# Attention and an expert layer on one core: a new planner for the instruction order, and the expert rows in two groups

## The chip, the cores and the metric

The kernel runs on one core of one Trainium2 chip. The metric is the device time of one execution in microseconds (us). The kernel before takes 981.07 us, the median of 3 runs (979.69 to 981.55).

## What is computed

Attention over 4 batches, 8 heads, 1152 keys and 64 channels, with neighbouring query rows averaged in pairs (576 query rows a batch), and then a two-layer expert network on the 2304 rows of 512 channels:

```python
q_pool = q.reshape(B, H, S // 2, 2, D).mean(axis=3)
scores = np.matmul(q_pool, k.transpose(0, 1, 3, 2)) / np.sqrt(D)
attn = softmax(scores)
x = np.matmul(attn, v).transpose(0, 2, 1, 3).reshape(B * 576, H * D)
h = x @ w_in                                   # 512 -> 2048
g = np.where(h > 0, h, np.exp(np.minimum(h, 0)) - 1)
out = g @ w_out                                # 2048 -> 512
```

Every fp32 operand of a matmul is held as a high and a low fp16 half under a power-of-two scale, and a product is the sum of three partial products.

## The kernel before

**Units, pairs and steps.** A batch is a unit, and a unit has four pairs of heads. A pair has nine steps: four tiles of 128 rows for each head, and a ninth step with the last 64 rows of both heads. So there are 36 steps a unit and 144 in all. One step (`attention`, from line 626) is a chain: the scores on PE (L643, L649) into the only PSUM tile `s`; the scale and row maximum on DVE (L655); the exponential on ACT (L661); the row sum and its reciprocal (L666, L669); the high half of the probabilities on POOL (L672) or ACT (L680); the low half on DVE (L675); and a DMA transpose from SP's queue that carries both halves from an `ep` buffer (3 of them) into a `pT` buffer (2 of them) (L699). In a "slow" step ACT makes the high half and POOL makes the low half in two instructions (L683, L689); every second one of the first 40 steps is slow. After two steps PE multiplies with V (L736, L742), and ACT and DVE add the result into `x32` (L754, L759), of which there is one buffer.

**Preparation of a pair** (`prep`, L336): loads of q, k and v, absolute maxima on ACT, a maximum over the partitions with two small PE matmuls (`across`, L314), the halves, a DMA transpose of q into `qT` (L439) with three copies behind it (L445, L448), and one of k into `kT` (L451). `kT`, `qT` and `v16` have two buffers each, so a pair can be prepared while one other pair is in work.

**Weights** (`weights`, L494): 8 groups of w_in and 8 of w_out arrive as 64-bit words. DVE decodes the two halves of a group in six instructions (L520, L524, L529, each for both halves), ACT finds the maximum, and the halves are scaled and split (L574, L577, L583).

**Experts** (`experts`, L773), once for each unit, when its last step is in `x32`: two maxima over `x32` (L786), one scale for all 576 rows, the halves of x (L821, L826), and then two row groups of 256 and 320 rows. In each, the first layer is 192 matmuls (L850), with ACT, POOL and DVE behind each result (L858 to L897), and the second layer is 96 or 144 matmuls (L917), with the output from SP's queue (L938).

**What orders the work.** Nothing runs in the order of the source. `Plan.run` (L79) is a list scheduler that runs when the program is built. Every task has an engine, an assumed duration and a key (a due time from the constants `CFG`); some have a second engine that they may go to. The planner keeps a time at which each engine is free, gives the free engine the ready task with the lowest key for which the buffers can be had, and so writes out a fixed order for PE, DVE, ACT, POOL and SP. The chip follows that order on each engine and waits on semaphores where the assumed times are wrong. A DMA has an assumed hold of the queue and a latency, and PE has a factor of 1.45 for unit 0.

Of the kernel before, what the change touches and what calls it, by code (L numbers as in the profile page):

```python
# [17 lines left out]
CFG = dict(LOADS=39538, PLM=2, NS=40, WI0=17116, WIT=12317, WO0=235211, WOT=4483, T0=4000, T1=2284, M0=8135, M1=33164, KS=15043, KM=7701, KE=39223, KH=2922, KL=-6882, KV=6859, KN=7241, KX=17067, KO=35556, PEN=0, W0L=-22914, WIN=1000, PD=2498,  # L18
)

# [17 lines left out]
class Plan:  # L38


    LAT = {"PE": 55.0, "DVE": 35.0, "ACT": 35.0, "POOL": 100.0, "DMA": 0.0}
# [37 lines left out]
    def run(self):  # L79
# [7 lines left out]
        free = {e: 0.0 for e in engines}  # L87
        wait = {e: [] for e in engines}
        events = [0.0]
# [5 lines left out]
        now = 0.0  # L95
        while done < len(self.tasks):
            if not events:
                left = sorted((t for t in self.tasks if t.end is None), key=lambda t: (t.key, t.n))
                raise RuntimeError("no task can be placed: " + "; ".join(
                    f"{t.eng} {t.emit.__name__} {t.left} {[(b.tag, b.slot) for b in t.bufs]}" for t in left[:12]))  # L100
            now = heapq.heappop(events)
            while events and events[0] <= now:
                heapq.heappop(events)
            again = True
            while again:
                again = False
                for e in engines:
                    if free[e] > now:
                        continue
                    best = None  # L110
                    for t in sorted((t for t in wait[e] if t.ready <= now), key=lambda t: (t.key, t.n)):
                        if e != t.eng:
                            ahead = sum(
                                o.dur for o in wait[t.eng]
                                if o.eng == t.eng and o.ready <= now + CFG["WIN"] and (o.key, o.n) < (t.key, t.n)
                            )
                            if now + t.ways[e][0] + CFG["PEN"] > max(free[t.eng], now) + ahead + t.dur:
                                continue
# [14 lines left out]
                    hold, lat = t.dur if isinstance(t.dur, tuple) else (t.dur, self.LAT[e])  # L133
                    free[e] = now + hold
                    t.start, t.end = now, now + hold + (lat if e == "DMA" else 0.0)
                    heapq.heappush(events, free[e])
                    heapq.heappush(events, t.end)
                    for kid in t.kids:
                        kid.left -= 1
                        extra = 60.0 if e == "DMA" else self.LAT[kid.eng]  # L140
                        kid.ready = max(kid.ready, t.end + extra)
                        if kid.left == 0:
                            for o in kid.ways:
                                wait[o].append(kid)
                        heapq.heappush(events, kid.ready)
                    order.append(t)
                    done += 1
                    again = True
        self.span = now
# [12 lines left out]
def attention_moe_kernel(  # L162
# [37 lines left out]
    pool("sm", 4, [128, 16], F32)  # L200
# [6 lines left out]
    pool("us", 2, [128, 16], F32)  # L207
# [4 lines left out]
    pool("wm", 2, [128, 4], F32)  # L212
# [10 lines left out]
    def act(n):  # L223
        return 0.9 * n + 190.0

    def actp(n):
        return 0.85 * n + 130.0

    def dve(n):
        return 1.2 * n + 200.0  # L230

    def dvp(n):
        return 1.07 * n + 170.0

    def pol(n):
        return 0.8 * n + 460.0

    def pol2(n):
        return 2.0 * n + 330.0

    def mm(n, cold=False):
        return (n / 1.55 if cold else n / 2.4) + 14.0

    LOADS, PLM = CFG["LOADS"], CFG["PLM"]
# [24 lines left out]
    for u in units:  # L269
        u.first = len(steps)  # L270
        u.t0 = now
        for p in range(NP):
            pr = Rec()
            pr.u, pr.p, pr.i, pr.t0 = u, p, len(pairs), now
            pr.steps = []
            pairs.append(pr)
            jobs = [(h, t) for h in range(2) for t in range(u.nt)] + ([(None, u.nt)] if u.lo else [])
            for h, t in jobs:
# [4 lines left out]
                now += CFG["T0"] if u.i == 0 else CFG["T1"]  # L283
        u.t1 = now
# [29 lines left out]
    def across(src, n, key, after, bufs, take):  # L314
# [13 lines left out]
        t1 = plan.add("PE", 300.0, key, turn, after, [xp] + bufs)  # L328
        t2 = plan.add("DVE", 600.0, key, most, [t1], [xp, xr])
        t3 = plan.add("PE", 350.0, key, back, [t2], [xp, xr])  # L330
        return plan.add("DVE", 700.0, key, lambda: take(xp.ap[:, 256:256 + n]), [t3], [xp] + bufs)
# [4 lines left out]
    def prep(pr, t0, t1):  # L336
# [35 lines left out]
        def halves(n, kh, kl, dst_h, dst_l, src, j, after, bufs):  # L372
# [3 lines left out]
            return plan.add("DVE", dve(n), kl, f, [h], bufs, [("POOL", pol(n) + pol2(n), g)])  # L376
# [33 lines left out]
        tq = plan.add("DMA", (1600.0, 2500.0), lk - 10.0, load_q, (), [q32])  # L410
# [4 lines left out]
        if old is None:  # L415
# [4 lines left out]
            tk = plan.add("DMA", (1500.0, 2500.0), lk, load(k, k32), (), [k32])  # L420
            tv = plan.add("DMA", (1500.0, 2500.0), lk + 1, load(v, v32), (), [v32])
# [33 lines left out]
        qt = plan.add("DMA", (1400.0, 2500.0), key[8], q_t, [ql], [qn, qT])  # L455
        qw = plan.add("DMA", (1000.0, 2000.0), key[9], q_lo, [qt], [qT])
        pr.qs = plan.add("DMA", (500.0, 2000.0), key[9], q_hi, [qw], [qT])
        if old:
            pr.kdone = [plan.add("DMA", (1500.0, 2500.0), lk + 2, plain(k_f, lambda: old[0]), [old[4]], [kT])]
            pr.vdone = [plan.add("DMA", (1500.0, 2500.0), lk + 3, plain(v_f, lambda: old[1]), [old[5]], [v16])]  # L460
            return
        kl = halves(1152, key[6], key[7], k_h, k_l, k_s, 1, [sc, sums[2]], [kn, k32, sm])
        pr.kdone = [plan.add("DMA", (2500.0, 2500.0), key[9], k_t, [kl], [kn, kT])]
        pr.vdone = [halves(1152, key[11], key[12], v_h, v_l, v_s, 2, [sc], [v16, v32, sm])]
        if sum(o.b == b for o in units) > 1:
            kd = dr.tile([128, 2 * S], F16, name=f"kd{p}")
            vd = dr.tile([128, 2 * S], F16, name=f"vd{p}")
            kw = plan.add("DMA", (1500.0, 2500.0), key[15], plain(lambda: kd, k_f), pr.kdone, [kT])
            vw = plan.add("DMA", (1500.0, 2500.0), key[15], plain(lambda: vd, v_f), pr.vdone, [v16])
            kept[b, p] = (kd, vd, sm, pr.sc, kw, vw)  # L470

    for pr in pairs:
        if pr.i == 0:
            prep(pr, -9000.0, 0.0)
        else:
            prev = pairs[pr.i - 1]
            prep(pr, prev.t0 - 2000.0, pr.t0 - 4000.0)
# [16 lines left out]
    def weights(which, g, t0, t1):  # L494
# [5 lines left out]
        for s in range(2):  # L500
# [7 lines left out]

            lds.append(plan.add("DMA", (1350.0, 2700.0), CFG["W0L"] + s if g + which == 0 else t0 - 14000.0 + s, load, (), [raws[s]]))

# [5 lines left out]
        def dec():  # L516
            us_ = [u.ap.bitcast(U32) for u in us]
            w = [raw_words(r) for r in raws]
            for s in range(2):
                nc.vector.tensor_scalar(  # L520
                    us_[s], w[s][:, :, 1], 5, 2, op0=ALU.logical_shift_left, op1=ALU.logical_shift_right
                )
            for s in range(2):
                nc.vector.scalar_tensor_tensor(  # L524
                    out=us_[s], in0=w[s][:, :, 1], scalar=0xC0000000, in1=us_[s],
                    op0=ALU.bitwise_and, op1=ALU.bitwise_or,
                )
            for s in range(2):
                nc.vector.scalar_tensor_tensor(  # L529
                    out=dst(s), in0=w[s][:, :, 0], scalar=29, in1=us_[s],  # L530
                    op0=ALU.logical_shift_right, op1=ALU.bitwise_or,
                )

        def osum():
            for s in range(2):
                to = mo[:, 2 * g + s:2 * g + s + 1] if which else wm[0].ap[:, s:s + 1]
# [444 lines left out]
```

## Time and profile before

| | us |
|---|---|
| median of 3 runs | 981.07 |
| the profiled execution's own time | 977.62 |
| its span, first to last instruction | 975.8 |
| end of the attention steps of units 0, 1, 2, 3 | 278.7, 483.7, 687.2, 871.0 |
| from the end of unit 3's steps to the end of the span | 104.8 |

Times in the profile count from the span's first instruction. An end of a unit's steps is read where DVE starts the second of the two maxima over `x32` (L786), which needs the last result of the unit. A busy share averages over stages with different limits, so the stages between these times are read one by one. PEclk is the granted clock of TensorE, where 1.00 is 2.4 GHz and 0.5 is 1.2 GHz.

### The profile page before, as it was taken

What the parts mean: (1) busy time and instruction counts of PE and PEld (TensorE: products, weight loads), DVE (VectorE), ACT (ScalarE), POOL (GpSimd) and SP (SyncE); (2) the same over time, 40 slices, a digit from 0 to 9 for tenths busy, and PEclk for the clock granted to TensorE, in tenths of its full rate; (3) what the DMA queues carried; (4) which work ended last, traced back from release to release, by engine and by line L of the source; (5) the groups of instructions that cost most, each with busy time, mean ns of one, the idle gap of its engine ahead of it and who ended that gap; (6) DMA issues with size and microseconds to landing.
All of it is one profiled execution on the core that took longest, in us unless ns stands there. A gap on an engine that the chain in (4) does not pass through costs nothing.

```text
span 975.8 us, 14669 instructions
## 1 busy us (share of the span) xinstructions
PE 745.6 (76%) x5271; PEld 416.6 (43%) x5271; DVE 747.6 (77%) x1200; ACT 627.9 (64%) x1093; POOL 519.0 (53%) x422
## 2 busy tenths in 40 slices
PE   0364464654258989889769997989698999999997
PEld 0122132322126645544346444544365455458563
DVE  5797989899789978788778776887877789845150
ACT  3576786666476868776557666865677778734260
POOL 4373867477579963783247634771276247505130
PEclk9998575556659999999979998999799999999999
DMA  7599899899956989999977989799888698640000
GB/s 238 134 212 228 190 199 254 184 227 222 271 109 126 177 156 184 171 177 184 183 148 137 206 163 193 132 203 190 172 174 172 132 176 135 123 94 7 22 2 27
DMA packets 434057, 156.94 MB, mean 161 GB/s; under 512 B 395840, under 2 KB 414272, under 8 KB 433984
## 3 DMA queue, kind: packets, MB, share of 16 engines
q1 hardware_dynamic: 433984, 156.01, 78.6%
q8 instruction: 41, 0.67, 0.3%
q14 instruction: 32, 0.26, 0.1%
HBM read 45.09 MB, written 4.72 MB: 51 GB/s over the span
## 4 chain that ended last, share of the span: by engine, by line
PE 32%; DMA 21%; DVE 12%; POOL 6%; issue 2%; ACT 2%; SPq 2%; DVEq 0%; POOLq 0%; ACTq 0%
DMA pT<-ep 16%; PE r L917 12%; PE r L850 8%; DVE ep L655 5%; PE r L736 4%; PE s L643 3%; DVE ep L675 3%; PE r L742 2%; PE s L649 2%; DMA kT<-kn 2%; DMA qT<-qn 1%; DMA q<-in_q_dram 1%; POOL ep L672 1%; ACT ep L661 1%; DVE tmp L871 1%
## 5 line engine op out<-in xcount | busy, mean ns | idle before, releaser
L655 DVE TENSOR_SCALAR_CACHE_REDUCE ep<-s,sm 128x1152 f32<-128x1152 f32 x133 | 188.0, 1414 | 80.1 <-DMA pT<-ep 52.2
L661 ACT ACTIVATE ep<-ep,nm 128x1152 f32<-128x1152 f32 x133 | 166.5, 1252 | 98.7 <-DVE ep L655 86.1
L850 PE MATMUL r<-x,wi 128*128 128x256 f16 (+1 forms) x1536 | 201.9, 290 | 9.3 <-DVE x L759 3.1
L643 PE MATMUL s<-kT,qT 128*128 128x512 f16 (+3 forms) x480 | 122.3, 370 | 113.1 <-DVE ep L655 88.9
L675 DVE SCALAR_TENSOR_TENSOR ep<-ep,nm 128x1152 f16<-128x1152 f32 x118 | 193.5, 1642 | 9.2 <-POOL ep L672 6.3
L917 PE MATMUL r<-wo,g 128*128 128x512 f16 (+1 forms) x864 | 174.8, 380 | 0.5 <-DVE tmp L871 0.3
L850 PEld LDWEIGHTS <-wi 128*128 128x128 f16 x1536 | 148.1, 99 | 60.1 <-issue 18.4
L736 PE MATMUL r<-pT,v 128*128 128x256 f16 (+1 forms) x864 | 100.8, 268 | 61.7 <-DMA pT<-ep 49.4
L672 POOL TENSOR_SCALAR ep<-ep,nm 128x1152 f16<-128x1152 f32 x52 | 73.2, 1408 | 104.2 <-DVE nm L669 102.5
L866 POOL TENSOR_SCALAR tmp<-tmp,us 128x320 f32<-128x320 f32 (+1 forms) x96 | 79.6, 830 | 90.4 <-ACT tmp L861 85.6
L680 ACT ACTIVATE ep<-ep,nm 128x1152 f16<-128x1152 f32 x81 | 101.3, 1251 | 31.0 <-DVE nm L669 30.7
L643 PEld LDWEIGHTS <-qT 128*128 128x128 f16 (+1 forms) x480 | 44.8, 106 | 174.8 <-issue 135.3
L917 PEld LDWEIGHTS <-g 128*128 128x128 f16 (+1 forms) x864 | 73.1, 100 | 88.9 <-issue 9.3
L736 PEld LDWEIGHTS <-v 128*128 128x128 f16 x864 | 68.8, 105 | 93.6 <-issue 47.7
L871 DVE SCALAR_TENSOR_TENSOR tmp<-r,wk,tmp 128x320 f32<-128x320 f32 (+1 forms) x96 | 58.0, 611 | 33.4 <-POOL tmp L866 33.2
L649 PE MATMUL s<-kT,qT 64*128 64x512 f16 (+3 forms) x480 | 80.8, 370 | 0.0
L754 ACT ACTIVATE x<-r,sm 64x256 f32<-64x256 f32 (+1 forms) x96 | 39.9, 415 | 47.3 <-PE r L742 45.4
L893 POOL TENSOR_SCALAR g<-tmp 128x320 f16<-128x320 f32 (+1 forms) x55 | 46.7, 850 | 35.8 <-DVE tmp L871 33.4
L742 PE MATMUL r<-pT,v 128*64 128x256 f16 (+1 forms) x864 | 65.5, 274 | 0.0
L858 ACT ACTIVATE tmp<-r 128x320 f32<-128x320 f32 (+1 forms) x96 | 46.3, 484 | 26.5 <-PE r L850 25.0
L889 POOL TENSOR_TENSOR g<-tmp,g 128x320 f16<-128x320 f32 (+1 forms) x54 | 56.8, 1058 | 4.8 <-ACT g L885 3.0
L861 ACT ACTIVATE tmp<-tmp,us 128x320 f32<-128x320 f32 (+1 forms) x96 | 57.7, 609 | 1.5
(136 smaller groups left out, 1029.2 us busy)
## 6 DMA issues: line engine op xcount, KB each, us to landing
k<-in_k_dram SPq DMA_DIRECT2D x16, 576.0 KB, 4.9
v<-in_v_dram SPq DMA_DIRECT2D x16, 576.0 KB, 4.9
q<-in_q_dram SPq DMA_DIRECT2D x32, 256.0 KB, 3.4
qT<-qT SPq DMA_DIRECT2D x48, 144.0 KB, 2.8
g<-in_moe_w_in_dram SPq DMA_DIRECT2D x13, 512.0 KB, 5.4
g<-in_moe_w_out_dram SPq DMA_DIRECT2D x13, 512.0 KB, 4.8
out_dram<-tmp SPq DMA_DIRECT2D x16, 256.0 KB, 2.5
pT<-ep SPq DMA_TRANSPOSE x133, 4.8
```

The source lines that it names most:

```text
L643: nc.tensor.matmul(s.ap[rows, c, 0:n], pr.qT.ap[:, 0, j, rows], keys[c], start=True, stop=False, skip_group_check=True,)
L649: nc.tensor.matmul(s.ap[rows, c, 0:n], pr.qT.ap[r, 1, j, rows], keys[c][r], start=False, stop=True, skip_group_check=True,)
L655: nc.vector.tensor_scalar(e_(), s.ap.rearrange("p a b -> p (a b)")[:, 0:S], pr.sm.ap[:, 12:13], None, op0=ALU.mult, op1=ALU.min, accum_out ...
L661: nc.scalar.activation(out=e_(), in_=e_(), func=AF.Exp, bias=nm.ap[:, 0:1], scale=-1.0, accum_out=nm.ap[:, 2:3],)
L672: nc.gpsimd.tensor_scalar(p_(0), e_(), nm.ap[:, 3:4], 1.0, op0=ALU.mult, op1=ALU.mult)
L675: nc.vector.scalar_tensor_tensor(out=p_(1), in0=e_(), scalar=nm.ap[:, 3:4], in1=p_(0), op0=ALU.mult, op1=ALU.subtract)
L680: nc.scalar.activation(out=p_(0), in_=e_(), func=AF.Copy, scale=nm.ap[:, 3:4])
L736: nc.tensor.matmul(x.ap[:, os], vt[:, order[c]].rearrange("p e d -> p (e d)"), pT.ap[:, c, cs], start=(c == 0), stop=False, skip_group_che ...
L742: nc.tensor.matmul(x.ap[r0:r0 + 64, os], vt[:, order[c], 0], pT.ap[:, NCH + c, cs], start=False, stop=(c >= NCH - 2), skip_group_check=True,)
L850: nc.tensor.matmul(hp.ap[:, f * n:(f + 1) * n], w[:, a, c, (f0 + f) * 128:(f0 + f + 1) * 128], x16.ap[:, e, c, g0:g0 + n], start=(i == 0), ...
L866: nc.gpsimd.tensor_scalar(en.ap[:, :m], en.ap[:, :m], -1.0, us.ap[:, 5:6], op0=ALU.add, op1=ALU.mult)
L917: nc.tensor.matmul(op.ap[r0:r0 + tn, :], gt[qd].ap[:, a, fi, o:o + tn], w_out16(f // 2)[:, e, f % 2, :], start=(i < 128 // tn), stop=(i >= ...
```

## The change

**The planner.** `Plan.run` becomes an event simulation. A task's remaining work is worked down at a rate: DVE and POOL slow each other down while DVE runs a task marked `Port` (rate 0.72 or 0.55), PE runs at 0.57 in a window after little use, and a DMA (`Move`) holds the queue for a first duration and the transfer path for a second one, with 2 us of flight; the transposes of `pT` and `kT` hold the queue until the path is free. Nearly all assumed durations and all `CFG` constants are replaced, with own constants for unit 0 (names that end in 0). On the chip none of this is executed: it changes the order on the engines and the choice of engine where a task has two.

**Steps.** The slow steps become every fourth of the first 36 (`PLM0=4`, `NS0=36`), and none later (`PLM=0`). In each unit the last two pairs are interleaved: four steps of pair 2 (the first two tiles of both heads), four of pair 3, then the five others of pair 2 and the five others of pair 3.

**Experts in two groups with own scales.** `experts` is called for each group; group 0 (256 rows) depends only on the tiles 0 and 1 of each head, so on step 26 of 36. Each group has its own maxima, `across` and scale; `us` gets a third buffer. Both groups share the one `x16` buffer.

**Weights.** The decode is a task for each half; it waits for the low half of the first pair's keys (`first_keys`). The maxima go straight to their columns, and `wm` is now only a token of which there is one, so that one group's maxima and scale are done before those of the next.

```diff
-CFG = dict(LOADS=39538, PLM=2, NS=40, WI0=17116, WIT=12317, ...
+    LOADS=84962, WI0=22119, WIT=12449, WO0=250979, WOT=5600, T0=3996, T1=1105, M0=11183,
...
+    KE0=53762, KH0=-8737, KL0=-4366, KV0=9486, KX0=32985, PLM0=4, NS0=36, PLM=0,
+    M2=18442, DP=0, PA=-86, PB=4000,
...
+            if d is not None and p is not None and isinstance(d.dur, Port):
+                return 0.72 if isinstance(p.dur, Port) else 0.55
+            return 1.0
...
+                    if e == "DMA":
+                        moved = max(now + rest[e], max(moved, now) + t.dur.far)
+                        heapq.heappush(landing, (moved + self.FLIGHT, t.n, t))
+                        rest[e] = (moved - now if t.dur.hold else rest[e]) + 90.0
...
+        early = [(h, t) for h in range(2) for t in range(2)]
+        late_ = [(h, t) for h in range(2) for t in range(2, u.nt)] + [(None, u.nt)]
+        turns = [(pr, early + late_) for pr in mine[:-2]] + [(pr, early) for pr in mine[-2:]] + [(pr, late_) for pr in mine[-2:]]
...
+            td = plan.add("DVE", Port(2000.0), t0 + s, dec, [lds[s], first_keys], [raws[s], us[s]] + to)
...
-        slow = st.i < CFG["NS"] and st.i % PLM == PLM - 1
+        every = K("PLM", u)
+        slow = every and st.i % every == every - 1 and (u.i > 0 or st.i < CFG["NS0"])
...
-        tt = plan.add("DMA", (CFG["PD"], 2200.0), t0, ptr, [tl], [ep, pT])
+        tt = plan.add("DMA", Move(2690.0, 2150.0, True), t0, ptr, [tl], [ep, pT])
...
+        u.xdone[0 if st.h is not None and st.t < 2 else 1].append(plan.add("DVE", 400.0 if n == 256 else 490.0, ...
...
-    def experts(u, t0, t1):
-        us, x16 = plan.buf("us"), plan.buf("x16")
+    def experts(u, gi, t0, t1):
+        us, x16 = plan.buf("us"), u.x16
+        g0, n = u.groups[gi]
...
-        if u.i + 1 < len(units):
-            experts(u, u.t1 + CFG["M0"], units[u.i + 1].t1 + CFG["M1"])
...
+        u.x16 = plan.buf("x16")
+        ends = units[u.i + 1].ready if u.i + 1 < len(units) else [u.t1 + 100000.0, u.t1 + 200000.0]
+        experts(u, 0, u.ready[0] + CFG["M0"], u.ready[1] + CFG["M2"])
+        experts(u, 1, u.ready[1] + CFG["M2"], ends[0] + CFG["M1"])
```

## Rows read from the trace of the kernel before

**Rows 1.** The page, part 1: busy us, share of the span, instructions.

```profile
PE 745.6 (76%) x5271; PEld 416.6 (43%) x5271; DVE 747.6 (77%) x1200; ACT 627.9 (64%) x1093; POOL 519.0 (53%) x422
```

**Rows 2.** The page, part 2: busy tenths in 40 slices, and granted clock.

```profile
PE   0364464654258989889769997989698999999997
...
DVE  5797989899789978788778776887877789845150
...
PEclk9998575556659999999979998999799999999999
```

**Rows 3.** Windows by stage: busy us (instructions) of each engine, clock, DMA share, GB/s.

```profile
core 0: us, PE busy (x) PEld busy (x) DVE busy (x) ACT busy (x) POOL busy (x), PEclk, DMA share, GB/s
50.00:279.00 229.00, 116.91 (x702) 56.32 (x702) 204.32 (x341) 149.32 (x264) 144.38 (x77) 0.67 0.98 215
279.00:484.00 205.00, 177.19 (x1317) 100.23 (x1315) 172.95 (x262) 151.43 (x263) 133.45 (x116) 0.96 0.89 167
484.00:687.00 203.00, 174.76 (x1287) 98.54 (x1287) 161.43 (x254) 138.97 (x245) 106.74 (x95) 0.94 0.89 172
687.00:871.00 184.00, 166.95 (x1267) 96.17 (x1265) 143.23 (x227) 127.03 (x217) 90.22 (x83) 0.96 0.80 150
871.00:975.80 104.80, 99.86 (x670) 61.56 (x667) 33.93 (x63) 39.32 (x70) 24.28 (x35) 1.00 0.05 16
```

**Rows 4.** Timeline of DVE where units 0, 1 and 2 end: start, us, instruction.

```profile
278.69 0.75 DVE L786 TENSOR_REDUCE us<-x 128x1 f32<-128x576 f32 x1
483.68 0.75 DVE L786 TENSOR_REDUCE us<-x 128x1 f32<-128x576 f32 x1
687.22 0.74 DVE L786 TENSOR_REDUCE us<-x 128x1 f32<-128x576 f32 x1
```

**Rows 5.** Timeline of the end, all engines.

```profile
861.09 1.42 DVE L675 SCALAR_TENSOR_TENSOR ep<-ep,nm 128x1152 f16<-128x1152 f32 x1 [1.37 <-POOL ep L672]
...
870.95 0.75 DVE L786 TENSOR_REDUCE us<-x 128x1 f32<-128x576 f32 x1
...
876.81 21.17 PE L850 MATMUL r<-x,wi 128*128 128x256 f16 x192
...
918.54 26.30 PE L850 MATMUL r<-x,wi 128*128 128x320 f16 x192
...
970.95 0.69 ACT L930 ACTIVATE tmp<-r,us 64x512 f32<-64x512 f32 x1 [4.67 <-PE r L917]
```

**Rows 6.** Timeline of the start, all engines.

```profile
13.76 1.22 POOL L306 TENSOR_SCALAR kn<-k,sm 128x1152 f16<-128x1152 f32 x1 [12.46 <-DMA g<-in_moe_w_in_dram]
...
15.19 0.41 DVE L520 TENSOR_SCALAR tmp<-g 128x512 uint32<-128x512 uint32 x1
...
20.03 1.37 SPq L439 DMA_TRANSPOSE qT<-qn  x1
...
20.41 4.78 DVE L363 SCALAR_TENSOR_TENSOR kn<-k,sm,kn 128x576 f16<-128x576 f32 x2
...
35.38 1.12 PE L643 MATMUL s<-kT,qT 128*128 128x512 f16 x3 [6.60 <-DMA qT<-qT]
```

**Rows 7.** Groups by line and form, 50 to 279 us: busy us, mean ns | idle before.

```profile
L689 POOL TENSOR_TENSOR ep<-ep 128x1152 f16<-128x1152 f32 x13 | 36.7, 2820 | 11.6 <-ACT ep L686 11.1
...
L675 DVE SCALAR_TENSOR_TENSOR ep<-ep,nm 128x1152 f16<-128x1152 f32 x12 | 23.9, 1991 | 0.0
...
L520 DVE TENSOR_SCALAR tmp<-g 128x512 uint32<-128x512 uint32 x21 | 15.6, 771 | 2.9 <-ACT tmp L537 2.9
```

**Rows 8.** The page, part 5: the maxima of the scores, whole span.

```profile
L655 DVE TENSOR_SCALAR_CACHE_REDUCE ep<-s,sm 128x1152 f32<-128x1152 f32 x133 | 188.0, 1414 | 80.1 <-DMA pT<-ep 52.2
```

**Rows 9.** The page, part 6: KB each, median us to landing.

```profile
qT<-qT SPq DMA_DIRECT2D x48, 144.0 KB, 2.8
...
pT<-ep SPq DMA_TRANSPOSE x133, 4.8
...
kT<-kn SPq DMA_TRANSPOSE x16, 5.8
```

More of the change, by code (lines that the diff above doesn't have):

```diff
@@ L86, in run @@
         engines = ("PE", "DVE", "ACT", "POOL", "DMA")
-        free = {e: 0.0 for e in engines}
         wait = {e: [] for e in engines}
-        events = [0.0]
+        busy = {e: None for e in engines}
+        rest = {e: 0.0 for e in engines}
+        landing, events = [], []
         for t in self.tasks:
@@ L95, in run, with shares, finish @@
         now = 0.0
-        while done < len(self.tasks):
[L97 to L103, printed above, removed]
+        turn, used, cold, moved = self.WINDOW, 0.0, True, 0.0
+        def shares():
+            d, p = busy["DVE"], busy["POOL"]
+            if d is not None and p is not None and isinstance(d.dur, Port):
+                return 0.72 if isinstance(p.dur, Port) else 0.55
+            return 1.0
+        def finish(t, at):
+            t.end = at
+            for kid in t.kids:
+                kid.left -= 1
+                kid.ready = max(kid.ready, at + self.TAIL[t.eng] + (30.0 if t.eng == "DMA" else self.LAT[kid.eng]))
+                if kid.left == 0:
+                    for o in kid.ways:
+                        wait[o].append(kid)
+                    heapq.heappush(events, kid.ready)
+        while done < len(self.tasks):
             again = True
@@ L107, in run @@
                 for e in engines:
-                    if free[e] > now:
+                    if busy[e] is not None:
                         continue
@@ L112, in run @@
                         if e != t.eng:
-                            ahead = sum(
+                            ahead = rest[t.eng] if busy[t.eng] is not None else 0.0
+                            ahead += sum(
                                 o.dur for o in wait[t.eng]
@@ L132, in run @@
                     t.eng = e
[L133 to L145, printed above, removed]
+                    t.start = now
+                    busy[e] = t
+                    rest[e] = float(t.dur)
+                    if e == "DMA":
+                        moved = max(now + rest[e], max(moved, now) + t.dur.far)
+                        heapq.heappush(landing, (moved + self.FLIGHT, t.n, t))
+                        rest[e] = (moved - now if t.dur.hold else rest[e]) + 90.0
                     order.append(t)
@@ L326, in back @@
             nc.tensor.matmul(xp.ap[:, 256:256 + n], ones[0:n].to_broadcast([n, 128]), xr.ap[0:n, 4:4 + n], start=True, stop=True)
[L328 to L331, printed above, removed]
+        t1 = plan.add("PE", 200.0, key, turn, after, [xp] + bufs)
+        t2 = plan.add("DVE", 440.0, key, most, [t1], [xp, xr])
+        t3 = plan.add("PE", 310.0, key, back, [t2], [xp, xr])
+        return plan.add("DVE", 600.0, key, lambda: take(xp.ap[:, 256:256 + n]), [t3], [xp] + bufs)
     kept = {}
@@ L834, in experts, with xhi, xlo @@
-        for gi, (g0, n) in enumerate(u.groups):
+        def xhi():
+            nc.scalar.activation(
+                out=x16.ap[:, 0, :, g0:g0 + n], in_=u.x32.ap[:, :, g0:g0 + n], func=AF.Copy, scale=us.ap[:, 2:3]
+            )
+        def xlo():
+            nc.vector.scalar_tensor_tensor(
+                out=x16.ap[:, 1, :, g0:g0 + n], in0=u.x32.ap[:, :, g0:g0 + n], scalar=us.ap[:, 2:3],
+                in1=x16.ap[:, 0, :, g0:g0 + n], op0=ALU.mult, op1=ALU.subtract,
+            )
+        th = plan.add("ACT", act(NP * n), t0, xhi, [txs], [x16, u.x32, us])
@@ L835, in experts @@
+        xready = plan.add("DVE", dve(NP * n), t0, xlo, [th], [x16, u.x32, us])
+        if True:
             gt = [plan.buf(*(("h", "g") if n <= 256 else ("g",))) for _ in range(4)]
```

252 lines of the change are left out of this document (143 added, 109 removed).

## The prediction

> **What bounds the kernel now.** I read the stages first, because the whole-span shares (PE 76%, DVE 77%) name no engine [rows 1]. The forty slices show three regimes: DVE nearly full and PE half empty up to slice 11, both high up to slice 34, and then PE alone with DVE near nothing [rows 2]. The windows, cut where the units end, put numbers to it [rows 3, 4]. From 50 to 279 us DVE is busy 204 of 229 us (89%) while PE has 117 at a granted clock of 0.67, nearer to its lower level of 1.2 GHz than to 2.4: DVE bounds unit 0. In units 1 to 3 PE is busy 86, 86 and 91% and DVE 84, 80 and 78%: no engine is full, each waits in turn, and the order decides. The last 104.8 us are PE alone (99.9 busy, DVE 33.9). There PE runs, back to back, the first and second layer of unit 3's group 0 and then of group 1 [rows 5]. This work could not start earlier because its one scale needs the last row of unit 3.
>
> The sum is made against the profiled execution, 977.62 us with a span of 975.8. It lies 3.5 us under the median of 981.07, and I add that at the end. A difference of about 0.2% (2 us) is what a measurement of this kernel can tell from none.
>
> **Term 1, the end.** Group 0 of unit 3 takes PE from 876.81 to 918.54, 41.7 us [rows 5]. After the change it needs step 26 of 36 only. If all of it ran before the last step, the tail would be the 5.9 us from the last maximum to the first matmul, 52.4 us for group 1 (918.54 to 970.95) and 4.9 to the end: 63.1 in place of 104.8, a gain of 41.7, the upper end. But PE must hold it beside the last ten steps. These last 184 x 10/36 = 51 us, less 5.9 for the scale of group 0 leaves 45. PE's attention work in unit 3 is 167 busy less one expert pass of 94 (876.81 to 970.95) = 73, so 20 in ten steps. 20 + 41.7 is 62, and 17 us hang over the end; they cover the 5.9 us of group 1's scale, so the tail is 17 + 52.4 + 4.9 = 74 and the gain 31, the lower end. I take -33, near the lower end, because PE's row for unit 3 (91%) is nearly as full as the row in which PE runs alone (95%).
>
> The Trainium skill, page "Perfetto Trace Analysis", section "Identifying the Most-Contended Engine", says that matmul busy time is a poor measure of room on PE and that the weight-load share is the better one. That share is 52% in unit 3 [rows 3], which read alone would leave PE half free and make this term -42. The trace disagrees with that reading here: in the tail, where PE is surely the limit, the weight-load share is only 59% [rows 3], so 52% is 89% of full.
>
> In the other units the same step moves group 0 from the next unit into its own. In units 1 and 2 as much leaves as comes. In unit 0 the matmuls go where PE is half idle, at no cost on PE; if that cover were gone they would cost 42 us, or twice that at the lower clock.
>
> **Term 2, the start.** The low half of the first keys is ready to start at 13.76 + 1.22 = 14.98 but runs on DVE at 20.41, behind decode work [rows 6]. The decode now waits for it. The first scores at 35.38 can come up to 5.4 us earlier. The other end is 0: DVE bounds unit 0, and the displaced decode has to be done there too. I take -4, because DVE also waits idle just ahead of the first scores. Behind the decode's new wait stand only the maxima and splits of the weights, which group 0 needs some 26 steps later.
>
> **Term 3, low halves moved to DVE.** Slow steps fall from 20 to 9, so 11 low halves move from POOL (2.82 us each [rows 7]) to DVE, nine of them in unit 0, where DVE is the bound. One costs DVE 1.42 when POOL is quiet [rows 5] and 1.99 as the mean of twelve in unit 0 [rows 7]: +16 to +22. Against this POOL loses 11 x 2.8 us and as many normalisations, and gains 11 shorter high halves; I estimate a fifth of its 144 us in unit 0. Slowed DVE work shows in rows 7: the low halves (12 x 0.57 = 7 us) and the first decode instruction (0.77 against 0.41 in rows 6, 21 x 0.36 = 8). A fifth of these 15 is 3, and I estimate double for the groups not shown: -6. Net +10, with ends +22 and 0.
>
> The Trainium skill, page "SBUF — State Buffer", section "Who interferes with whom", has VectorE and GpSimd share one port pair as an exclusive lock, taken by a VectorE instruction with two SBUF inputs. By it each move would free the port of 2.82 - 1.42 = 1.4 us, 15 us in all, and this term would be +1. The trace agrees as to who is slowed: L655, with its input in PSUM, stays at 1.41 in the mean [rows 8], and L675, with two SBUF inputs, does not [rows 5, 7]. By both rules together the sum would be 917, still in the forecast's own range.
>
> **Term 4, vector work out of the tail, and one more scale a unit.** DVE's 33.9 us in the tail serve both groups [rows 3]; about 12 belong to group 0 and move to where DVE is busier. They cost 0 to 12 us; I take +4, as unit 3 leaves DVE 22% free. The second scale repeats about 1.7 us of small DVE instructions four times, with two PE matmuls that other PE work queues behind: 0 to +7, I take +3.
>
> **Term 5, the order itself.** The longest wait on DVE is for `ep`, that is for a `pT` transpose to land: 52 us in all [rows 8]. A planner that knows how long a transpose holds the queue can cut this, and one that is wrong can double it. At best units 1 to 3 run DVE (173 + 161 + 143 = 477 us busy in 592) at 90%, about its share in unit 0, which is 531 us: -61. At worst +26. I take half of the 52 us, -26, because this wait is the one that the new durations describe; the other waits I leave as they are.
>
> **What costs nothing.** The token `wm`, now single, makes the eight w_in groups run one behind the other, in some 170 us before group 0 can use them; if that cover were gone, group 0 of unit 0 would come later into a stretch where PE is half idle. The one `x16` makes group 0 of a unit wait for the first layer of the last unit's group 1, which has 26 steps of time. The DMAs stay the same in number and size; on SP's queue (one transpose a step, 4.8 us to landing [rows 9]) only their order changes.
>
> **Sum.** -33 - 4 + 10 + 4 + 3 - 26 = -46. 977.6 - 46 = 931.6, and with 3.5 for the median 935.
>
> **Rivals.**
> A, the order gives its best: term 5 is -61, so 935 - 35 = 900. For it speaks that no engine is over 91% in units 1 to 3; against it, that PE and DVE are both over 78% there and wait on each other.
>
> B, group 0 does not come forward: the planner puts it behind the attention steps, or buffers for its results are not free. Term 1 falls away: 935 + 33 = 968. For it speaks that PE is 91% busy in unit 3.
>
> C, slower: interleaved pairs keep both buffers of `kT` and `qT`. Now a buffer comes free nine steps before it is needed, and scores wait for a transposed query only once, at the start (6.60 us [rows 6]). After the change pair 3 has four steps of time (4 x 203/36 = 22.6 us) and the next unit's first pair five (28): seven places. From the issue of the query transpose to the first scores the start took 35.38 - 20.03 = 15.4 us with no `pT` transpose ahead [rows 6]. Up to three of those at 4.8 ahead of its parts [rows 9] make 30. At 30 the stall is 7.4 x 4 + 2 x 3 = 36 us and eats most of the gain; it decides from a chain of about 32 us on. At 34 it is 11.4 x 4 + 6 x 3 = 64, and the time 999. Against it: SP's queue can take these parts first.
>
> D, the change does not do what it says, as the fixed order is only another wrong guess: near 981.
>
> **Chances.** Forecast (915 to 952) 0.50, A (885 to 915) 0.23, B and a partial C (952 to 979) 0.14, D 0.03, C in full 0.10. The range, 892 to 974, leaves out the best quarter of A (0.06), the end of B (0.02), D and C (0.13). Alone, the forecast's own range is 915 to 952. Faster by over 0.2%: 0.50 + 0.23 + 0.14 = 0.87; within 0.2%: 0.03; slower: 0.10.
>
> **What would show it.** Right: the first matmuls of a group 0 (256 columns) stand before the unit's last maximum over `x32`; the time from the last result to the end falls from 105 to between 63 and 75; the first scores stand near 31; 135 low halves on DVE; the wait of L655 on `pT` is near 26. Wrong: scores that wait for `qT` or `kT` in each unit (C), unit 0 longer than 279 by more than 15 us (term 3), or a tail still above 90 (B).

## The result, and the profile after

The changed kernel takes 957.89 us, the median of 4 runs (955.32 to 960.3), against 981.31 (4 runs): a ratio of 0.9766, 95% interval 0.9748 to 0.9784. It is faster by 23 us; forecast were 46. The profiled execution takes 955.32 us with a span of 953.5, so it stands 2.6 us under its median, and 22.3 us of span went.

Part 1 of the page of the changed kernel answers to [rows 1]:

```profile
PE 755.5 (79%) x5283; PEld 423.7 (44%) x5283; DVE 750.8 (79%) x1267; ACT 646.2 (68%) x1114; POOL 388.8 (41%) x360
```

DVE does as much as before (747.6), POOL 130 us less. The windows by stage, cut where the last result of each unit is added, answer to [rows 3]; the columns are the same:

```profile
50.00:266.10 216.10, 133.61 (x861) 70.71 (x861) 198.54 (x344) 157.90 (x275) 97.25 (x61) 0.74 1.02 218
266.10:480.00 213.90, 178.79 (x1278) 101.54 (x1277) 183.43 (x300) 155.90 (x274) 116.23 (x109) 0.91 0.85 167
480.00:688.80 208.80, 192.90 (x1441) 110.59 (x1440) 165.73 (x272) 143.53 (x248) 88.99 (x89) 0.98 0.82 163
688.80:865.30 176.50, 159.26 (x1202) 91.87 (x1201) 142.66 (x234) 136.23 (x225) 60.41 (x65) 0.95 0.86 162
865.30:953.50 88.20, 80.28 (x471) 44.77 (x468) 25.22 (x52) 29.92 (x58) 12.19 (x21) 0.96 0.04 14
```

[rows 3] is cut a little later, where the last maximum starts. Cut at the last add, units 1 to 3 of the kernel before are:

```profile
276.80:483.70 206.90, 177.36 (x1317) 100.36 (x1317) 174.78 (x268) 153.31 (x265) 135.27 (x117) 0.95 0.89 167
483.70:685.10 201.40, 172.86 (x1277) 97.83 (x1278) 159.84 (x253) 137.37 (x241) 106.05 (x95) 0.94 0.89 172
685.10:870.90 185.80, 168.75 (x1276) 96.81 (x1275) 145.06 (x226) 128.93 (x221) 91.21 (x84) 0.96 0.80 151
```

The attention ends at 865.3 and not at 870.9: only 5.6 us earlier, although unit 0 ends 10.7 earlier (266.1 against 276.8). Units 1 and 2 are 214 and 209 us long, 7 longer each than before, and unit 3 is 9 shorter. Part of this is work that moved: DVE's 96 decode instructions all ran in unit 0 before, and now 18 of them, 13.8 us, run in unit 1. The tail is 88.2 us, not 104.9, and not the 63 to 74 of the prediction. The timeline of the end shows why (it answers to [rows 5]; L858 is the maximum, L396 the first small matmul of a scale, L922 the first layer, L989 the second):

```profile
821.88 0.42 DVE L858 TENSOR_REDUCE us<-x 128x1 f32<-128x256 f32 x1
...
838.87 2.79 PE L922 MATMUL r<-x,wi 128*128 128x256 f16 x24
...
866.02 0.47 DVE L858 TENSOR_REDUCE us<-x 128x1 f32<-128x320 f32 x1
...
874.15 15.70 PE L989 MATMUL r<-wo,g 128*128 128x512 f16 x72
...
889.69 0.27 PE L396 MATMUL r<-ident,us 128*1 128x128 f32 x1
...
894.55 27.99 PE L922 MATMUL r<-x,wi 128*128 128x320 f16 x188 [0.36 <-DVE x L898]
...
922.38 26.18 PE L989 MATMUL r<-wo,g 128*128 128x512 f16 x144
```

Group 0's first layer now starts ahead of the end, at 838.87, but 17 us behind its maximum. Group 1's maximum is done at 866.5, and its small matmul runs at 889.69, directly behind the last matmul of group 0's second layer. From there to 892.97 PE has next to nothing, then four matmuls, and the 188 from 894.55 on take 27.99 us, 149 ns each, where 192 took 26.30 [rows 5], 137 each. Windows of this stretch show that the 149 is a mean of two rates:

```profile
889.70:892.97 3.27, 0.64 (x5) 0.39 (x4) 1.50 (x10) 2.05 (x2) 0.00 (x0) 0.92 0.22 80
892.97:899.00 6.03, 5.67 (x21) 3.00 (x21) 1.84 (x2) 1.00 (x2) 0.54 (x1) 0.50 0.00 0
900.00:922.40 22.40, 22.40 (x167) 16.13 (x166) 13.35 (x27) 18.16 (x40) 8.03 (x15) 1.00 0.00 1
```

After 3.3 us in which PE is busy 0.64, the granted clock is 0.50 (1.2 GHz) up to 899.00, with 270 ns a matmul; from 900 on it is 1.00 (2.4 GHz), with 137. So of the tail 24.4 us are the overhang of group 0 (865.3 to 889.7), and some 6.6 are lost at the start of group 1: about half in the pause, half at the lower clock.

The same waiting stands at the start of unit 2. Timeline of unit 1's group 1 there (L898 is the low half of x, L808 the first product with V of unit 2, L727 the maximum of a step):

```profile
482.72 0.47 DVE L858 TENSOR_REDUCE us<-x 128x1 f32<-128x320 f32 x1
...
492.18 1.42 DVE L727 TENSOR_SCALAR_CACHE_REDUCE ep<-s,sm 128x1152 f32<-128x1152 f32 x1 [1.35 <-DMA pT<-ep]
...
500.32 0.27 PE L396 MATMUL r<-ident,us 128*1 128x128 f32 x1
...
505.50 2.62 DVE L898 SCALAR_TENSOR_TENSOR x<-x,us,x 128x1280 f16<-128x1280 f32 x1 [0.86 <-ACT x L893]
507.54 1.16 PE L808 MATMUL r<-pT,v 128*128 128x256 f16 x9
...
515.88 1.42 DVE L727 TENSOR_SCALAR_CACHE_REDUCE ep<-s,sm 128x1152 f32<-128x1152 f32 x1 [3.75 <-DMA pT<-ep]
```

From maximum to small matmul it is 17.6 us. No step's maximum starts between 492.18 and 515.88. There is one `x32`, and to the planner a product with V is one of its users; so the order has unit 2's first product behind the tasks that read unit 1's rows, L898 the last of them (on the chip the two overlap by 0.6 us). `pT` fills, then `ep`, and L727 waits for a transpose. L898 is done 28.2 us behind unit 1's last add; in the kernel before L826, its like, was done 19.5 us behind it.

The two longest such gaps are not filled alike. Windows from one maximum to the next, at the start of units 1 and 2:

```profile
275.41:298.70 23.29, 11.04 (x54) 6.42 (x54) 21.95 (x45) 10.21 (x20) 6.33 (x5) 0.57 0.66 159
492.18:515.88 23.70, 22.22 (x144) 12.07 (x143) 13.00 (x28) 9.35 (x14) 3.87 (x5) 1.00 0.52 113
```

In unit 1 DVE is busy 22.0 of 23.3 us, 12.6 of it with the decode that moved there. In unit 2 PE is busy 22.2 of 23.7 us with layers of the experts, and DVE waits.

The whole-span wait that term 5 spoke of did shrink, from 52.2 us [rows 8] to 32.2:

```profile
L727 DVE TENSOR_SCALAR_CACHE_REDUCE ep<-s,sm 128x1152 f32<-128x1152 f32 x132 | 186.4, 1412 | 49.7 <-DMA pT<-ep 32.2
```

My theory T: the scale of group 1 carries the due time of group 1's matmuls, and group 0's second layer, always due earlier, goes ahead of it on PE, once in the tail and at three boundaries. Rivals: units 1 and 2 are long because PE is full with moved work (R), the interleaved pairs wait for `kT` or `qT` (C), or the planner is the whole gain.

### The profile page after: what moved, and what is told of

The parts are those of the page before. It is cut to its first block, busy times and chain, and to the rows that moved or that the text cites. A ratio compares the mean times of both kernels' runs of the same rounds, so it can differ in the third digit from the quotient of the medians.

```text
span 953.5 us, 14727 instructions
## 1 busy us (share of the span) xinstructions
PE 755.5 (79%) x5283; PEld 423.7 (44%) x5283; DVE 750.8 (79%) x1267; ACT 646.2 (68%) x1114; POOL 388.8 (41%) x360
## 4 chain that ended last, share of the span: by engine, by line
PE 32%; DVE 22%; DMA 16%; ACT 5%; issue 5%; POOL 2%; SPq 0%; DVEq 0%; ACTq 0%; POOLq 0%
DMA pT<-ep 13%; PE r L989 11%; PE r L922 10%; DVE ep L727 7%; DVE ep L747 5%; PE s L715 4%; PE r L808 3%; PE s L721 2%; ACT ep L733 2%; PE r L814 2%; DVE tmp L943 1%; DVE tmp L601 1%; DVE v L440 1%; POOL tmp L938 1%; DVE x L831 1%
## 5 line engine op out<-in xcount | busy, mean ns | idle before, releaser
L727 DVE TENSOR_SCALAR_CACHE_REDUCE ep<-s,sm 128x1152 f32<-128x1152 f32 x132 | 186.4, 1412 | 49.7 <-DMA pT<-ep 32.2
L922 PE MATMUL r<-x,wi 128*128 128x256 f16 (+1 forms) x1536 | 207.3, 294 | 12.6 <-DVE x L831 6.1
L747 DVE SCALAR_TENSOR_TENSOR ep<-ep,nm 128x1152 f16<-128x1152 f32 x125 | 193.2, 1548 | 10.7 <-POOL ep L744 5.3
L922 PEld LDWEIGHTS <-wi 128*128 128x128 f16 x1536 | 149.6, 100 | 65.0 <-issue 24.4
L989 PE MATMUL r<-wo,g 128*128 128x512 f16 (+1 forms) x864 | 174.0, 380 | 0.0
L744 POOL TENSOR_SCALAR ep<-ep,nm 128x1152 f16<-128x1152 f32 x43 | 59.9, 1393 | 204.6 <-DVE nm L741 187.8
L752 ACT ACTIVATE ep<-ep,nm 128x1152 f16<-128x1152 f32 x89 | 111.4, 1252 | 35.9 <-DVE nm L741 35.6
L808 PE MATMUL r<-pT,v 128*128 128x256 f16 (+1 forms) x855 | 103.3, 273 | 23.0 <-DMA pT<-ep 9.5
L938 POOL TENSOR_SCALAR tmp<-tmp,us 128x320 f32<-128x320 f32 (+1 forms) x96 | 73.2, 764 | 117.8 <-ACT tmp L933 113.7
L989 PEld LDWEIGHTS <-g 128*128 128x128 f16 (+1 forms) x864 | 74.3, 100 | 86.8 <-issue 7.5
L808 PEld LDWEIGHTS <-v 128*128 128x128 f16 x864 | 71.1, 107 | 57.8 <-issue 26.9
L943 DVE SCALAR_TENSOR_TENSOR tmp<-r,wk,tmp 128x320 f32<-128x320 f32 (+1 forms) x96 | 57.4, 608 | 19.4 <-POOL tmp L938 19.3
L826 ACT ACTIVATE x<-r,sm 64x256 f32<-64x256 f32 (+1 forms) x96 | 39.8, 414 | 20.2 <-PE r L814 18.9
L831 DVE SCALAR_TENSOR_TENSOR x<-r,sm,x 64x256 f32<-64x256 f32 (+1 forms) x96 | 39.0, 407 | 17.0 <-ACT x L826 15.7
```

What stands on the lines that cost most here:

```text
L727: nc.vector.tensor_scalar(e_(), s.ap.rearrange("p a b -> p (a b)")[:, 0:S], pr.sm.ap[:, 12:13], None, op0=ALU.mult, op1=ALU.min, accum_out ...
L747: nc.vector.scalar_tensor_tensor(out=p_(1), in0=e_(), scalar=nm.ap[:, 3:4], in1=p_(0), op0=ALU.mult, op1=ALU.subtract)
L752: nc.scalar.activation(out=p_(0), in_=e_(), func=AF.Copy, scale=nm.ap[:, 3:4])
L808: nc.tensor.matmul(x.ap[:, os], vt[:, order[c]].rearrange("p e d -> p (e d)"), pT.ap[:, c, cs], start=(c == 0), stop=False, skip_group_che ...
L922: nc.tensor.matmul(hp.ap[:, f * n:(f + 1) * n], w[:, a, c, (f0 + f) * 128:(f0 + f + 1) * 128], x16.ap[:, e, c, g0:g0 + n], start=(i == 0), ...
L938: nc.gpsimd.tensor_scalar(en.ap[:, :m], en.ap[:, :m], -1.0, us.ap[:, 5:6], op0=ALU.add, op1=ALU.mult)
```

## The experiments

**Group 1's scale due earlier, in unit 3 alone.**

```diff
-        txr = plan.add("DVE", 90.0, t0, xtop, txm, [us])
+        tk = u.ready[1] if gi == 1 and u.i == 3 else t0
+        txr = plan.add("DVE", 90.0, tk, xtop, txm, [us])
```

The other tasks of the scale and the halves get `tk` too.

> Only unit 3's group-1 scale gets an earlier due time (when its rows are complete, not when group 0's second layer is done). Theory T (the two small matmuls of that scale stand on PE behind all of group 0's second layer, 889.69 us after the change, although the maximum is ready at 866.5): the idle piece from 889.7 to 894.5 ahead of group 1's first matmul goes, and with it the slower matmuls behind it; the tail of 88 us becomes 80 to 83 and the time 949 to 953. Rival R (PE would only wait elsewhere, as DVE and ACT are busy with group 0's results): within 2 us of 957.9.

Measured: 951.89 us, ratio 0.9725 (0.9698 to 0.9753), 6 us less than the change, or 4 by the ratios (the kernel before took 979.0 us beside this one and 981.3 beside the change). On every engine the order is that of the change up to 868.97 us, so only the tail can differ by the edit: it is 82.1 us, 6.1 less. (The attention ends at 868.3, 3.0 later than in the profiled execution of the change; with the same order this is scatter.) Timeline of its end (its lines count one higher), then the window of its tail:

```profile
869.01 0.47 DVE L859 TENSOR_REDUCE us<-x 128x1 f32<-128x320 f32 x1
...
871.96 0.27 PE L396 MATMUL r<-ident,us 128*1 128x128 f32 x1
...
894.85 24.61 PE L923 MATMUL r<-x,wi 128*128 128x320 f16 x180
```

```profile
868.30:950.50 82.20, 77.19 (x471) 43.64 (x468) 24.27 (x51) 30.16 (x59) 12.82 (x21) 1.00 0.04 15
```

The small matmul stands 3 us behind its maximum, group 1 follows group 0 without a gap, a matmul takes 137 ns again, and the granted clock of the tail is 1.00. T holds for the tail.

**The same in all units.**

```diff
+        tk = u.ready[1] - 20000.0 if gi == 1 else t0
```

> The group-1 scale of all four units gets an earlier due time. Theory T (the one x32 buffer is held until group 1's scale and halves are done, which is what stops the steps for 23, 24 and 16 us at the start of units 1, 2 and 3): these gaps fall to 15 or less, units 1 and 2 fall from 214 and 209 us towards 205, and the time is 933 to 945. Rival R (units 1 and 2 are longer than before because PE is full with the moved expert work): only the tail gains, 949 to 953, with units 1 and 2 as long as after the change. Every new due time also makes a new order, so some us either way are the order's own.

Measured: 939.59 us, ratio 0.9602 (0.9580 to 0.9625), 18 us less than the change, 16 by the ratios. Its start of unit 2, then its windows from unit 1 on:

```profile
470.96 0.48 DVE L859 TENSOR_REDUCE us<-x 128x1 f32<-128x320 f32 x1
...
474.70 0.27 PE L396 MATMUL r<-ident,us 128*1 128x128 f32 x1
...
482.99 1.54 DVE L899 SCALAR_TENSOR_TENSOR x<-x,us,x 128x1280 f16<-128x1280 f32 x1
```

```profile
262.20:469.60 207.40, 170.73 (x1206) 96.25 (x1207) 184.92 (x294) 150.98 (x268) 118.26 (x107) 0.88 0.86 173
469.60:672.20 202.60, 189.54 (x1456) 110.82 (x1455) 163.27 (x273) 151.21 (x254) 91.73 (x92) 0.99 0.89 176
672.20:857.80 185.60, 171.84 (x1288) 99.24 (x1287) 150.16 (x241) 135.64 (x230) 75.95 (x76) 0.96 0.84 155
857.80:937.10 79.30, 74.21 (x442) 40.76 (x439) 23.58 (x49) 29.06 (x57) 9.96 (x18) 0.98 0.05 16
```

The longest gaps between two steps' maxima at the start of units 1, 2 and 3 are 14.5, 10.2 and 11.1 us, where they were 23.3, 23.7 and 16.3 after the change, and 12.6, 11.2 and 11.1 before it. L899 is done 14.9 us behind unit 1's last add, not 28.2. Units 1 and 2 are 207 and 203 us, 13 less together. Unit 3 is 185.6, 9 more, as PE has more of group 0 in it (1288 instructions, 1202 after the change); the tail is 9 us shorter for it. PE is busier in unit 2 (94%, 92% after the change) and the unit is shorter, and in unit 1 PE is at 82%: R falls. So the due time of the scale decides the gaps. That the hold is `x32`, and not another thing that the scale has, is read from the order and was not tried by itself.

**And group 0's scale in unit 3.**

```diff
-        tk = u.ready[1] - 20000.0 if gi == 1 else t0
+        tk = u.ready[1] - 20000.0 if gi == 1 else (u.ready[0] if u.i == 3 else t0)
```

> As the kernel with all group-1 scales early (939.6 us, tail 79), and in unit 3 group 0's scale is due as soon as its rows are complete too. After the change group 0's first matmul starts 17 us behind its maximum (821.9 to 838.9) and not 5.9 as I took it. Theory T (the tail is what PE still holds of group 0): this distance falls to 8 to 12 us, the tail to 72 to 77 and the time to 933 to 938. Rival R (PE is full before the end, so matmuls that start earlier only delay the attention): 938 to 942.

Measured: 937.83 us, ratio 0.9562 (0.9537 to 0.9586), 1.8 us less than the last.

```profile
810.19 0.40 DVE L859 TENSOR_REDUCE us<-x 128x1 f32<-128x256 f32 x1
...
822.79 4.27 PE L923 MATMUL r<-x,wi 128*128 128x256 f16 x24
```

The distance is 12.6 us, where T had 8 to 12, and the tail 77.0. The total is in T's range, but only 0.2 us under R's, and with intervals that touch it is no clear gain; the attention ends 0.9 us later, which speaks a little for R. It is the fastest version here and beats both kernels.

**The new planner without the groups.** The experts start after the last step, as before, and the pairs run one after the other.

```diff
-        turns = [(pr, early + late_) for pr in mine[:-2]] + [(pr, early) for pr in mine[-2:]] + [(pr, late_) for pr in mine[-2:]]
+        turns = [(pr, early + late_) for pr in mine[:-1]] + [(mine[-1], early), (mine[-1], late_)]
...
-        done = u.xdone[gi]
+        if gi == 0:
+            done = u.xdone[0] + u.xdone[1]
...
-        experts(u, 0, u.ready[0] + CFG["M0"], u.ready[1] + CFG["M2"])
-        experts(u, 1, u.ready[1] + CFG["M2"], ends[0] + CFG["M1"])
+        end = units[u.i + 1].t1 + 20000.0 if u.i + 1 < len(units) else u.t1 + 200000.0
+        start = u.t1 + 4000.0
+        mid = start + (end - start) * 0.45
+        experts(u, 0, start, mid)
+        experts(u, 1, mid, end)
```

> The new planner and its durations, with one scale for all 576 rows of a unit, the experts only after the unit's last step, and pair 2 finished ahead of pair 3. Theory T (the planner brings the attention forward by a few us and the grouping alone shortens the tail): the tail is 100 to 106 us as before, the attention ends at 855 to 872, the time is 962 to 980. Rival R (the planner is the whole gain): the time is 950 to 960.

Measured: 966.57 us, ratio 0.9860 (0.9825 to 0.9896), 12.4 us less than its kernel before (978.97). Its tail is 106.5 us:

```profile
860.40:966.90 106.50, 96.70 (x627) 60.42 (x627) 34.55 (x63) 39.86 (x73) 21.29 (x31) 0.96 0.04 13
```

T's ranges for the time and the attention hold, R's does not: the planner brings the attention forward by 10.5 us, and the groups as changed add 9 to that. The due times of the experts were set by hand here, so the planner alone may be worth more. Its 10.5 us come from units 0 and 1, which end at 469.6 (483.7 before); units 2 and 3 take 391 us, 3.5 more than before. Units 0 and 1 end at 469.6 with all scales early too, and at 480.0 in the change (483.1 and 476.0 in the two controls below): the boundary cost some 10 us there. With the scales early, the groups give 27 us of tail (106.5 to 79.3) and cost the attention nothing.

**The old planner with the groups**, and the same with the scales early.

```diff
+        u.x16 = plan.buf("x16")
+        ends = units[u.i + 1].ready if u.i + 1 < len(units) else [u.t1 + 50000.0, u.t1 + 100000.0]
+        experts(u, 0, u.ready[0] + 0.0, u.ready[1] + 20000.0)
+        experts(u, 1, u.ready[1] + 20000.0, ends[0] + 50000.0)
```

> The kernel before with its old planner, durations and constants, but with the two groups with own scales and the last two pairs interleaved. Theory T (the grouping shortens the tail, and the boundary between units costs some of it): the tail is 75 to 95 us, units 1 and 2 are 5 to 15 us longer than before each, the time is 965 to 990. Rival R (the grouping is the whole gain): 950 to 962.

> The old planner with the two groups (1010.1 us), with the group-1 scales early. Theory T (the hold of x32 over the boundary is a cost under either planner): units 1 and 2, 239 and 220 us, fall by 10 or more each, the time is 975 to 1000. Rival R (the old planner's loss has another cause: its assumed times do not fit the denser order): 1000 to 1020.

Measured: 1010.07 us, ratio 1.0326 (1.0297 to 1.0355), and 998.99, ratio 1.0197 (1.0154 to 1.0239). The tails are 73 and 72 us, the shortest of all, but the attention ends at 935 and 923:

```profile
277.60:516.80 239.20, 209.12 (x1480) 120.01 (x1479) 199.58 (x313) 161.14 (x284) 135.25 (x114) 0.93 0.73 145
516.80:737.00 220.20, 177.76 (x1292) 101.40 (x1291) 159.90 (x267) 141.34 (x246) 99.32 (x89) 0.90 0.79 157
737.00:935.30 198.30, 169.60 (x1273) 97.81 (x1271) 145.91 (x239) 134.53 (x228) 75.51 (x74) 0.95 0.77 147
935.30:1008.30 73.00, 67.18 (x406) 37.46 (x404) 20.23 (x46) 25.73 (x50) 11.63 (x20) 1.00 0.05 17
```

The first missed both ranges: units 1 and 2 are 32 and 19 us longer than before, where T had 5 to 15. The early scale gives 11 us here too, which puts the time into T's range, but units 1 and 2 (234 and 220) did not fall by 10 each, as T had it. Most of the old planner's loss has another cause, which stays open. The due times of the groups were set by hand and not fitted to the old planner; with these, the groups pay only with the new planner.

**Interleaved pairs alone**, added to the new planner with one scale (the `turns` line of the change put back).

> The new planner with one scale for a unit (966.6 us), with one thing added: the last two pairs interleaved as in the change, which brings nothing here and only shows what holding both buffers of kT and qT costs. Rival C of the prediction (a pair has four or five steps of time to be prepared in): scores wait for qT or kT, 36 to 64 us more, 1000 to 1030. Theory T (the preparation fits): no wait of scores on qT or kT beyond the one at the start, and the time is 960 to 975, the spread being that of a new order.

Measured: 970.50 us, ratio 0.9909 (0.9882 to 0.9936), 4 us more, which is within the scatter of an order (below). The waits on transposed queries in the whole span are 1.6 us:

```profile
PE s L716 <- DMA qT<-qT: 1.6, 2, 1.0
```

Rival C falls: a preparation fits into four or five steps.

**Plain pairs with the groups**, all scales early (the same `turns` line as in the one-scale kernel).

> The kernel with all group-1 scales early (939.6 us), with the pairs one after the other: group 0 is complete only at step 31 of 36 and not at 26. Theory T (the tail is what PE still holds): five steps (25 us) less for group 0 put most of its second layer and part of its first behind the attention, the tail grows from 79 to 95 or more and the time to 950 to 965. Rival R (interleaving costs the attention as much as it gives the tail): 935 to 945.

Measured: 971.63 us, ratio 0.9918 (0.9900 to 0.9936), 32 more. The tail is 90 us, 11 longer: T's way, but short of its 95. The other 21 are an attention that ends later (878.5), which T did not forecast, and the time is past its 965. So the interleaving is needed with these due times, and what it gives the attention is not explained.

**Slow steps as before.** `PLM0=2` in place of 4.

> The changed kernel with every second step of unit 0 slow, as before (18 in place of 9). Read on unit 0, up to its last result (266.1 us after the change). The prediction's term 3 (nine low halves more on DVE cost about 10 us there): unit 0 ends 5 to 15 us earlier, at 251 to 261. Rival (POOL's two long instructions slow DVE by as much as the moved work costs, as the port rule has it): unit 0 ends within 4 us of 266 or later. The total also holds a new order of all later units and is not read for this.

Measured: 965.51 us, ratio 0.9851 (0.9824 to 0.9878); unit 0 ends at 273.4, 7.3 us later (0.7 and 2.6 later in the two controls below), with DVE busy 208.8 us from 50 us on (198.5 after the change). Groups from 50 to 270 us, first of the changed kernel, then of this one:

```profile
L747 DVE SCALAR_TENSOR_TENSOR ep<-ep,nm 128x1152 f16<-128x1152 f32 x20 | 32.6, 1640 | 0.9 <-POOL ep L744 0.5 <-ACT ep L752 0.3
...
L600 DVE TENSOR_SCALAR tmp<-g 128x512 uint32<-128x512 uint32 x16 | 9.7, 605 | 0.2
```

```profile
L747 DVE SCALAR_TENSOR_TENSOR ep<-ep,nm 128x1152 f16<-128x1152 f32 x14 | 26.2, 1870 | 0.0
...
L600 DVE TENSOR_SCALAR tmp<-g 128x512 uint32<-128x512 uint32 x17 | 15.4, 906 | 0.0
```

With fewer long POOL instructions each low half takes 1.64 us, not 1.87, and the first decode instruction 0.61, not 0.91. The 10 us are not all the price of the slow steps: the longer stretch also holds work that the change has behind unit 0 (14 low halves of the weights, L649, where the change has 11). Over the whole span the work on DVE is nearly the same but for the nine low halves. Part 1 of this kernel's page:

```profile
PE 752.8 (78%) x5283; PEld 423.6 (44%) x5283; DVE 753.7 (78%) x1259; ACT 634.3 (66%) x1105; POOL 441.5 (46%) x386
```

That is 753.7 us of DVE without the nine and 750.8 with them (751.1 and 751.0 in the two controls): they cost DVE nothing. The low halves sum to 208.8 us with them and 199.6 without, and the first decode instructions to 16.9 and 23.3.

**The decode not held.** `[lds[s], first_keys]` becomes `[lds[s]]`.

> The changed kernel without the decode's wait for the first keys. Read on the start. The prediction's term 2 (the low half of the first keys stands behind decode work): the first scores move from 32.7 back to 34 to 36 us and unit 0's end by 0 to 4 us later. Rival (the query's chain sets the start, not the keys'): the first scores stay at 32 to 33. The total holds a new order of all later units and is not read for this.

Measured: 975.21 us, ratio 0.9950 (0.9925 to 0.9975). The low half of the first keys starts at 23.02 and the first scores at 41.27 us, 8.5 later than with the wait (32.74), and later than I expected; unit 0 ends 7.3 us later. The wait is worth 7 to 9 us to this planner.

**Two controls** with a due time changed by a little: `T1=1120` for 1105, and `KN=6622` for 6122.

> A control: the changed kernel with the due-time spacing T1 of units 1 to 3 at 1120 in place of 1105, which removes and adds no work. It shows how much of a run's total is the order's own. If an order alone moves little (under 3 us), the totals of the other experiments can be read as the parts' prices; if it moves 5 us or more, only stages and waits can.

> A second control of the same kind: the due time KN of the expert results at 6622 in place of 6122. Same reading: under 3 us from 957.9, or 5 and more; I expect the latter, up to 25 us slower, because the constants of the change fit one another.

Measured: 960.75 us, ratio 0.9798 (0.9771 to 0.9826), and 966.38, ratio 0.9856 (0.9827 to 0.9885): 3 and 8 us more than the change, with no work changed. So totals that differ by 8 us or less are not a part's price, and I read stages and waits. Both controls keep the gaps of 23 us and more at units 1 and 2, as does the kernel with unit 3's scale alone early; with the slow steps as before they are 26.1 and 19.4, with the decode not held 25.6 and 22.6. In the three kernels of the new planner with all scales early no gap at the start of a unit is over 14.5. So that reading does not hang on an order.

## Why the prediction was wrong

The sign was right, and -46 was twice what came. Against the forecast, by stages that end with a unit's last add, in us:

| | forecast | the change | all scales early |
|---|---|---|---|
| unit 0 (terms 2 and 3) | +6 | -10.7 | -14.6 |
| units 1 to 3 (terms 4 and 5) | -19 | +5.1 | +1.4 |
| tail (term 1) | -33 | -16.7 | -25.6 |

Units 1 to 3 hold 13.8 us of decode that unit 0 held before, so the first two rows are safest in sum: -13 forecast, -5.6 after the change. Two steps failed, term 1 and term 5, and the wrong sign of term 3 hid a part of it.

**Term 1 failed**, at the sentence that the overhang covers the 5.9 us of group 1's scale. It did not, because on PE the scale's small matmul was ordered behind the overhang. In the tail that cost 6 us (unit 3 alone), half of it at the lower clock. I had also priced the one more scale only as instructions (term 4, +3) and not as what it holds: until it is done, `x32` stays taken. Making all four early gave 16 to 18 us. The prediction named what is queued behind the new decode wait, and what costs nothing with `wm` and `x16`, but not what waits for the new scale. Its other half, the overhang, was too short by 7 us: 24 after the change (865.3 to 889.7) against 17, as group 0 started 17 us behind its maximum and not 5.9. The two make the 14 us from 74 to 88. With the scales early the groups gave 27 to 29 us (tails of 79.3 and 77.0 against 106.5), against 31 to 42 in the prediction.

**Term 5 failed** (-26): it had half of the wait for `pT` go out of units 1 to 3, and their time with it. The wait fell by 20 us over the whole span, near what was said, but 15 of that in units 0 and 1. In units 2 and 3, which have no decode in either kernel, it fell only from 28.3 us to 23.3, and the two take 385 us, 387 before. With the planner alone, which moves no group, it is 26.8 and they take 391: the new durations did not take this wait out of the later units. With all scales early it is 21.1 and they take 388, with 361 us of PE work in them where there were 342 before; whether the shorter wait made room for that work is not shown.

Groups of the maxima in units 2 and 3, first before (483.7 to 870.9 us), then after the change (480.0 to 865.3):

```profile
L655 DVE TENSOR_SCALAR_CACHE_REDUCE ep<-s,sm 128x1152 f32<-128x1152 f32 x69 | 97.6, 1414 | 42.4 <-DMA pT<-ep 28.3 <-PE s L649 11.4 <-PE r L850 1.0
L727 DVE TENSOR_SCALAR_CACHE_REDUCE ep<-s,sm 128x1152 f32<-128x1152 f32 x67 | 94.6, 1412 | 28.0 <-DMA pT<-ep 23.3 <-PE s L721 3.4 <-PE r L403 0.2
```

**Term 2** (-4): the first scores came 2.6 us earlier, 32.74 against 35.38 [rows 6]. Right in place, and near in size.

**Term 3** (+10) had the wrong sign. Undoing the move made unit 0 7.3 us longer. I had estimated the relief of DVE at 6 us from two rows; over the whole span DVE's busy time does not rise by the nine low halves (750.8 against 753.7 us), so the relief was as large as the cost. The Trainium skill, page "SBUF — State Buffer", section "Who interferes with whom", says that a VectorE instruction with two SBUF inputs and a GpSimd instruction that reads SBUF exclude each other. The low halves above, with two inputs, agree in direction (1.64 and 1.87 us); the decode instruction L600 has one input and is slowed as well, of which that sentence says nothing. The +1 that I drew from it was nearer than my +10.

**Term 4** (+7) did not show: with all scales early the attention ends 2.6 us ahead of the one-scale kernel, which has no second scale and keeps group 0's vector work in the tail. The scatter of an order, 3 to 8 us, is on that.

**Luck.** Terms 2 to 5 were -13 in sum, and the new planner without groups measured -12.4. This is no confirmation: that kernel has nothing of term 4, so -20 stands against it, and its gain is in units 0 and 1 and none in units 2 and 3, where term 5 had most of its own. With all scales early the attention ends 13.2 us earlier, the same sum once more out of other stages.

**Rivals.** C, the slower one, was wrong in place: the interleaving cost no wait. But a buffer held too long did decide, as the order has it: `x32` in place of `kT`. B was right in part: group 0 came forward for its first layer only. A's 900 was not reached: the best order here has 938.

## What to carry to other kernels

When work is cut into groups so that the first can start early, look at what the next group's first small step waits behind, on every engine, and give it a due time of its own; its price can be the time of the buffer it holds, and not its instructions. A wait that gets shorter is not yet a stage that gets shorter: read the stage's length. A list scheduler's order changes the time by itself, here by 3 to 8 us, so undo a part together with controls, and read stages. A part of a change can be worth nothing or less alone: the groups lost 3% with the old planner, with due times that were not fitted to it.

## What I had not expected of the hardware

A pause on PE of 3.3 us, three small matmuls of a scale in it, cost about as much again behind it: the granted clock fell to 0.50 (1.2 GHz) and stayed there up to 899.00, at 270 ns a matmul, before it was 1.00 again with 137 ns. Where the same small matmuls ran between group 0's, the clock of the tail stayed at 1.00.

And moving nine low halves from POOL to DVE cost DVE nothing: its busy time over the whole span was 750.8 us with them and 753.7 without, as its other instructions got shorter (the first decode instructions 16.9 us in sum and not 23.3).
